# Attention and a routed expert layer in one kernel: four stores per stretch moved one place, seven places for the first units' layers, list work moved inside a layer, and a different last scaling

## The chip, the cores and the metric

The kernel runs on one core of one Trainium2 chip. The metric is the device time of one execution in microseconds; of the kernel before there are three timed runs and one profiled execution.

## The reference, cut to what matters

```python
# attention, for each of 8 batches and 8 heads, 576 positions, 64 numbers per head
scores = q @ k.T / 8;  cum = cumsum(max(s, 0))
attn = softmax(where(causal, -1e9, scores + min(-(cum_i - cum_j), 0)))
x = (attn @ v) with the heads side by side                # 8 x 576 tokens of 512 numbers
# experts: 8 of them, w1[e] is 512 x 1024, w2[e] is 1024 x 512
logits = x @ w_gate
e[s] = argmax(logits[s]) if s == 0 or sigmoid(x[s] @ w_local) < 0.5 else e[s - 1]
out[s] = softmax(logits[s])[e[s]] * (max(x[s] @ w1[e[s]], 0) @ w2[e[s]])
```

Each token goes through one expert, and which one depends on the tokens before it in its batch.

## The kernel before, in words

**Attention** runs over 16 slots (`m` in `attention`). A slot takes two head pairs, `a` and `b`. TensorE first makes the scores of both (`ps`, line 1129); ScalarE turns them into exponentials `e` (line 1130), and GpSimd blanks the part above the diagonal (line 1113). TensorE then makes the diagonal blocks of the next slot's scores (`ph`, line 1147) and, for both pairs, the products with the values (`po` for `a`, `pb` for `b`, lines 1186 and 1198), each in two parts. VectorE divides each part by its sums (`recs`, `xb`, line 1208). `ph`, `po` and `pb` are many small matrix products of 64 columns; the scores are fewer and larger ones.

A slot has numbered places at which other work may be planned: 0 and 1 after the scores of `a` and `b`, 3 after the values of `a`, 4 after the values of `b`, 5 after VectorE's turning and weighting work. Four batches of tokens have been finished after eight slots, and so on: after every four slots a **group** of two batches is routed (`Router`: small products `lp`, line 231, and `pos`, line 316, and many small VectorE operations), and its 18 pieces of 128 half rows are stored into a table in DRAM, ordered by expert. Such a **store** is an indirect DMA that GpSimd issues (`put`, line 364), and ahead of each stands a one-element copy or memset into `gap` (lines 361 and 363) that makes it wait for something: in attention for a `recs` value of its place, later for the ScalarE result of its step. The table `STORES` says at which place of which slot each store stands. Stores of the third group that have no place there go into a list, `experts.puts`. The fourth group's 18 stores and 8 more (`pads`) join that list when the fourth group is routed (`late_rows`).

**Experts** runs 20 units of tokens of one expert each, `ORDER = "PPDDDDDDDDDDTDDRMDRR"`: most have 256 tokens, the last ones fewer. The phases are (1, 0), then (1, u), (2, u-1) for u = 1 to 19, then (2, 19), where (1, u) is the first layer of unit u and (2, u) its second. In `SPLIT` layers (both layers of D and R units, the second of P units) a layer is seven products of half size instead of eight, `layer_split`: products 1, 2, 6, 7, 5, 4, 3 in that order, with sums and differences of weights (`wt`, and in place `w1b`, `w2b`: `weight_first` to `weight_fourth`, line 618, VectorE) and of rows (`row_sums`, `row_fourth`, lines 663 to 669, GpSimd, or VectorE for the first layer of the first five units). After each product VectorE adds it up (`sa`, `sb`, `sc`, `hT`, `y`, line 712), and `at(0)` to `at(6)` run the work planned at that place. Such work, for other units, is planned with `job`, which cuts a place to the number of places a layer has. That number is in `steps`; for the second layer of a P unit it says 2, although that layer runs as a split one with seven places:

```python
steps = {"P": (FK, 2), "D": (7, 7), "R": (7, 7), "M": (2, 1), "T": (2, 1)}
plan(what, u, i if i == "pre" else min(i, steps[self.kind(u)][what - 1] - 1), lambda: f(*args))
```

At each place one store is taken from `experts.puts`. Which units hold whole doubles of which expert is computed in lists: `assign_early(0)` in attention slot 11 for the first `EARLY[0]` units, `assign_early(1)` in phase (1, 0) for the next `EARLY[1]`, `assign_doubles` in (1, 1), and `assign_rest`, a chain of 18 steps of one to five tiny VectorE operations, that starts with phase (2, 3). The rows of a unit are fetched from the table by SyncE (`fetch`, line 583), after every store that stands ahead of it in the program has landed, and the weights by SyncE (`load`, line 573). SyncE works in order.

At the end, the last layer's last product is added into `y` by VectorE, scaled by the gate `gi` on ScalarE (line 716) and stored with an indirect DMA from GpSimd (line 757).

Of the kernel before, what the change touches and what calls it, by code (L numbers as in the profile page):

```python
# [12 lines left out]
Alu = mybir.AluOpType  # L13
# [40 lines left out]
STORES = (((3, 5, 5, 5, 5), (3, 5, 5, 5, 5), (5, 5, 5, 5), (5, 5, 5, 5)), ((3, 5, 5, 5, 5), (3, 5, 5, 5, 5), (5, 5, 5, 5), (5, 5, 5, 5)),  # L54
          ((3, 4, 5, 5, 5, 5), (3, 5, 5, 5, 5)))
# [8 lines left out]
EARLY = (2, 3)  # L64
# [3 lines left out]
LOOK, REST_FROM, REST_STEP = 5, 8, 3  # L68
# [434 lines left out]
class Experts:  # L503
# [191 lines left out]
    def layer_split(self, u, layer, at):  # L695
# [48 lines left out]
        at(5, ins)  # L744
        p3 = self.product(u, layer, 3)
        add(c12, p3, s2)
        ins = last(c12, 0)
# [63 lines left out]
    def run(self, recs, wend, out_of):  # L811
# [61 lines left out]
        def late_rows():  # L873
            assert not self.puts
            router.ranks(last, self.banks)
            router.rows(last)
            router.gates(last, self.xb)
            self.puts += [lambda behind, c=c: router.scatter(last, c, behind=behind) for c in range(NC)]
            self.puts += router.pads()
# [8 lines left out]
        plan(1, 1, 2, lambda: loads(0), late_rows)  # L888
# [12 lines left out]
        steps = {"P": (FK, 2), "D": (7, 7), "R": (7, 7), "M": (2, 1), "T": (2, 1)}  # L901
# [5 lines left out]
        for u in range(end):  # L907
            if u >= 2:
                job(2, u - 2, "pre" if u > 2 else 1, turn_x, u)
            for layer in range(2):  # L910
                if not self.split(u, layer):
                    continue
                if layer:
# [6 lines left out]
                    if u < 2:  # L920
                        place = ((1, 1), (2, 0))[u] + ("pre",)
# [19 lines left out]

        def fetches():
            nonlocal fetched
            while fetched < min(end, turned + 2):
                stored = not self.puts
                if (1, 1, 2) in todo:
                    stored = stored and fetched < first
                elif fetched < first:
                    stored = True
                if not stored or self.table_of(*self.units[fetched][1][-1]) is None:  # L950
                    return
                self.fetch(fetched)
                fetched += 1
# [9 lines left out]
        def step(what, u):  # L963
            def at(i, ins=None):
                self.relu = ins or self.relu
                run_plan(what, u, i)
                if now >= REST_FROM and (7 * now + i) % REST_STEP == 0:
                    next(rest, None)
                if self.puts and (now or i > 2) and (now != 2 or i % 2 == 0):
                    self.puts.pop(0)(self.relu)  # L970
                fetches()
                free()
# [956 lines left out]
```

## Time and profile before

| | us |
|---|---|
| three timed runs | 697.51, 697.1, 700.85 |
| their median | 697.51 |
| profiled execution, time | 704.64 |
| its span from the first to the last instruction | 702.8 |
| TensorE busy | 678.5 |
| VectorE busy | 526.1 |
| GpSimd busy | 382.1 |
| ScalarE busy | 198.9 |

The profiled execution is 7.1 us over the median and 1.8 us over its own span. In its timeline the attention slots begin at 9.6 us and are some 11 us long, longer from the seventh on; the first expert phase begins at 212.0 us, (2, 0) at 242.6, (1, 2) at 257.1, and from there a phase takes some 12.3 us.

### The profile page before, as it was taken

How to read it: one execution, taken by the hardware profiler on the slowest of the kernel's cores; microseconds unless marked ns; L12 is line 12 of the kernel's file. 1: busy time of each engine (PE TensorE's matmuls, PEld its weight loads, DVE VectorE, ACT ScalarE, POOL GpSimd, SP SyncE). 2: the span in 40 equal slices, each digit the busy share in tenths (PEclk: the TensorE clock that was granted, in tenths of full speed). 3: DMA queues.
4: the chain of work that ended last, by engine and by line, in shares of the span. 5: the costliest groups of instructions: out<-in, count | busy, mean ns of one | idle time of the engine just before them, and what ended most of it. 6: DMA issues, size and time to landing. Idle time of an engine off the chain costs nothing.

```text
span 702.8 us, 19163 instructions
## 1 busy us (share of the span) xinstructions
PE 678.5 (97%) x7837; PEld 586.0 (83%) x7837; DVE 526.1 (75%) x979; ACT 198.9 (28%) x368; POOL 382.1 (54%) x547
## 2 busy tenths in 40 slices
PE   8999999989989989999999999999999999999995
PEld 6787877777768879999998999999777998679984
DVE  4655846876867588889989998887659686778763
ACT  4545436435421211212212122221211112111121
POOL 3552366766754768853654557456243482535742
PEclk9999999999999999999999999999999999999998
DMA  7664555656558589679876468166989898866001
GB/s 255 202 220 131 173 183 157 220 188 208 188 139 350 174 303 352 207 272 351 294 270 212 141 247 280 47 235 205 301 288 375 337 337 279 284 265 253 31 9 42
DMA packets 54968, 158.18 MB, mean 225 GB/s; under 512 B 11156, under 2 KB 31636, under 8 KB 49111
## 3 DMA queue, kind: packets, MB, share of 16 engines
q1 hardware_dynamic: 47751, 136.52, 57.2%
q0 software_dynamic: 6880, 20.10, 7.5%
q8 instruction: 64, 1.05, 0.6%
q14 instruction: 33, 0.27, 0.1%
q10 hardware_dynamic: 240, 0.25, 0.1%
HBM read 136.21 MB, written 20.85 MB: 223 GB/s over the span
## 4 chain that ended last, share of the span: by engine, by line
PE 88%; DVE 4%; issue 3%; DMA 3%; POOL 1%; ACT 1%; POOLq 0%; DVEq 0%
PE p L688 27%; PE p L692 26%; PE ps L1129 10%; PE po L1186 6%; PE pb L1186 6%; PE hp L782 4%; PE hp L773 2%; PE yp L805 2%; PE ph L1147 2%; PE lp L231 2%; DMA w1b<-in_w_dram 2%; PE po L1198 1%; DVE wt L618 1%; DMA qb<-in_q_dram 1%; PE pb L1198 1%
## 5 line engine op out<-in xcount | busy, mean ns | idle before, releaser
L692 PE MATMUL p<-w2b,hT 128*128 128x256 f32 (+1 forms) x720 | 164.9, 380 | 3.1 <-POOL gap L361 2.0
L692 PEld LDWEIGHTS p<-w2b,hT 128*128 128x128 f32 (+1 forms) x720 | 132.8, 187 | 25.7 <-issue 3.4
L688 PE MATMUL p<-xT,w1b 128*128 128x128 f32 (+1 forms) x1280 | 151.2, 275 | 1.3 <-DMA w1b<-in_w_dram 0.7
L688 PEld LDWEIGHTS p<-xT,w1b 128*128 128x128 f32 x1280 | 147.8, 192 | 4.3 <-issue 1.6
L1130 ACT ACTIVATE e<-ps 128x768 f32<-128x768 f32 (+1 forms) x96 | 76.9, 884 | 62.9 <-PE ps L1129 55.0
L757 POOL DMA_INDIRECT out_dram<-y,gi x38 | 44.7, 1175 | 82.2 <-ACT y L716 74.5
L716 ACT ACTIVATE y<-y,gi 128x256 f32<-128x256 f32 (+1 forms) x72 | 35.5, 506 | 167.5 <-DVE y L712 152.4
L717 ACT ACTIVATE hT<-hT 128x512 f32<-128x512 f32 (+1 forms) x64 | 39.0, 616 | 152.5 <-DVE hT L712 152.5
L1129 PE MATMUL ps<-qb,kb 64*128 64x384 f32 (+4 forms) x516 | 76.6, 441 | 2.3 <-DVE xb L1208 1.5
L669 POOL TENSOR_TENSOR hT<-hT,hS 128x512 f32<-128x512 f32 (+1 forms) x18 | 26.1, 1450 | 87.5 <-PE p L692 87.4
L1129 PEld LDWEIGHTS ps<-qb,kb 64*128 64x128 f32 x516 | 47.0, 186 | 29.5 <-ACT e L1130 8.7
L692 PE MATMUL p<-wt,hS 128*128 128x256 f32 (+1 forms) x288 | 68.0, 379 | 0.0
L364 POOL DMA_INDIRECT table<-xb,idx x54 | 58.2, 1077 | 14.6 <-issue 13.3
L688 PE MATMUL p<-xS,wt 128*128 128x128 f32 (+1 forms) x512 | 62.4, 275 | 0.0
L692 PEld LDWEIGHTS p<-wt,hS 128*128 128x128 f32 (+1 forms) x288 | 53.8, 187 | 8.4
L688 PEld LDWEIGHTS p<-xS,wt 128*128 128x128 f32 x512 | 59.7, 192 | 0.0
L1113 POOL TENSOR_SCALAR_AFFINE_SELECT e<-e 128x128 f32<-128x128 f32 (+1 forms) x96 | 33.6, 375 | 39.3 <-ACT e L1130 39.0
L1186 PE MATMUL pb<-vg,e 128*64 128x66 f32 x1280 | 41.3, 222 | 1.1 <-issue 1.0
L1186 PE MATMUL po<-vg,e 128*64 128x66 f32 x1280 | 42.0, 226 | 0.0
L1186 PEld LDWEIGHTS po<-vg,e 128*64 128x64 f32 x1280 | 39.7, 141 | 1.2
L1186 PEld LDWEIGHTS pb<-vg,e 128*64 128x64 f32 x1280 | 39.4, 138 | 1.7 <-issue 1.3
L665 POOL TENSOR_TENSOR hT<-hT 128x512 f32<-128x512 f32 (+1 forms) x18 | 36.4, 2020 | 0.0
(290 smaller groups left out, 998.3 us busy)
## 6 DMA issues: line engine op xcount, KB each, us to landing
w2b<-in_w_dram SPq DMA_DIRECT2D x23, 2048.0 KB
w1b<-in_w_dram SPq DMA_DIRECT2D x22, 2048.0 KB
va<-in_v_dram SPq DMA_DIRECT2D x32, 320.0 KB
kb<-in_k_dram SPq DMA_DIRECT2D x31, 288.0 KB
qb<-in_q_dram SPq DMA_DIRECT2D x31, 288.0 KB
xq<-table SPq DMA_DIRECT2D x60, 130.0 KB
w1b<-in_w_dram SPq DMA_DIRECT2D x4, 512.0 KB
xq<-table SPq DMA_DIRECT2D x12, 113.8 KB
```

The lines of the kernel that those rows point to most:

```text
L364: put = self.nc.gpsimd.indirect_dma_start(out=self.halves, in_=src, element_offset=0, in_offset=None, out_offset=bass.IndirectOffsetOnAxis ...
L665: on.tensor_tensor(a21, a11, a21, op=Alu.subtract)
L688: mm(ps[:, m * h : m * h + h], lhsT=b[:, k, m * P : m * P + P], rhs=a[:, k, :], start=m == 0 and k == 0, stop=m == FK // 2 - 1 and k == n - 1)
L692: mm(ps[:h, : D // 2], lhsT=a[:, k, :], rhs=b[:, k, :], start=k == 0, stop=k == n - 1)
L716: return nc.scalar.mul(to, to, gi[:h, r, 1:2]).ins
L717: return nc.scalar.activation(to, to, Act.Relu).ins
L757: put = nc.gpsimd.indirect_dma_start(out=self.out[:, :], out_offset=bass.IndirectOffsetOnAxis(ap=gi.bitcast(I32)[:m, n, 0:1], axis=0), in_ ...
L782: mm(ps, lhsT=self.ws[ls[0]][0][:, k, c * P : c * P + P], rhs=xT[:, k, :w], start=(k == 0), stop=(k == DK - 1))
L1113: nc.gpsimd.affine_select(out=ap, in_=ap, compare_op=Alu.is_ge, fill=0.0, base=base, pattern=n, channel_multiplier=-1)
L1129: mm(ps[:, h, at : at + z - a], lhsT=kb[d, key : key + P], rhs=qb[d, a:z], start=True, stop=True)
L1130: exps[n, u] = nc.scalar.activation(e[:, :, : WIDTH[u]], ps, Act.Exp, scale=scale).ins
L1186: of = mm(po[part][d, j - a, :], lhsT=weights_of(n, c, j, h), rhs=vgs[n % NV][:, c if j < 2 * G1 else G1 + c, h, :], start=(first and i == ...
```

## The change

Five things are edited.

- `STORES`: in the eight slots of groups 0 and 1, one store moves from place 5 to place 4. Group 2 had 11 stores in its two attention slots and now has 5, so 13 instead of 7 go to `experts.puts`, which then holds up to 39 instead of 33 over the phases. Stores are taken at all places of phase (1, 0) but the third, where before they were taken from the fourth on.
- `steps` says 7 for the second layer of P units, so work planned at later places of (2, 0) and (2, 1) stays there; two row sums get new places with it, and `loads(0)` moves from place 2 to place 1 of (1, 1).
- `EARLY` is (4, 1) instead of (2, 3), and `fetches` lets units 0 to 3 be fetched as soon as phase (1, 1) begins, without waiting for the list of stores to be empty.
- `assign_rest` advances at places 3 and 4 of each layer instead of at each third place counted through.
- In the very last layer ScalarE scales `s2` ahead, and one VectorE operation scales the last product and adds.

```diff
-STORES = (((3, 5, 5, 5, 5), (3, 5, 5, 5, 5), (5, 5, 5, 5), (5, 5, 5, 5)), ((3, 5, 5, 5, 5), (3, 5, 5, 5, 5), (5, 5, 5, 5), (5, 5, 5, 5)),
-          ((3, 4, 5, 5, 5, 5), (3, 5, 5, 5, 5)))
+STORES = (((3, 4, 5, 5, 5), (3, 4, 5, 5, 5), (4, 5, 5, 5), (4, 5, 5, 5)), ((3, 4, 5, 5, 5), (3, 4, 5, 5, 5), (4, 5, 5, 5), (4, 5, 5, 5)),
+          ((4, 5, 5, 5), (4,)))
...
-EARLY = (2, 3)
+EARLY = (4, 1)
...
-LOOK, REST_FROM, REST_STEP = 5, 8, 3
+LOOK, REST_FROM, REST_AT = 5, 8, (3, 4)
...
+        end = u == len(self.units) - 1
+        if layer and end:
+            nc.scalar.mul(s2, s2, gi[:h, 0, 1:2])
         p3 = self.product(u, layer, 3)
-        add(c12, p3, s2)
-        ins = last(c12, 0)
+        if layer and end:
+            ins = nc.vector.scalar_tensor_tensor(c12, p3, gi[:h, 0, 1:2], s2, Alu.mult, Alu.add).ins
+        else:
+            add(c12, p3, s2)
+            ins = last(c12, 0)
...
-        plan(1, 1, 2, lambda: loads(0), late_rows)
+        plan(1, 1, 1, lambda: loads(0))
+        plan(1, 1, 2, late_rows)
...
-        steps = {"P": (FK, 2), "D": (7, 7), "R": (7, 7), "M": (2, 1), "T": (2, 1)}
+        steps = {"P": (FK, 7), "D": (7, 7), "R": (7, 7), "M": (2, 1), "T": (2, 1)}
...
-                        place = ((1, 1), (2, 0))[u] + ("pre",)
+                        place = ((1, 1, "pre"), (2, 0, 2))[u]
...
+        def group_stored():
+            return len(self.puts) <= (0 if (1, 1, 2) in todo else NC + E)
+
         def fetches():
             nonlocal fetched
             while fetched < min(end, turned + 2):
-                stored = not self.puts
-                if (1, 1, 2) in todo:
-                    stored = stored and fetched < first
-                elif fetched < first:
-                    stored = True
-                if not stored or self.table_of(*self.units[fetched][1][-1]) is None:
+                stored = fetched < EARLY[0] or (fetched < first and group_stored()) or not ((1, 1, 2) in todo or self.puts)
+                if not now or not stored or self.table_of(*self.units[fetched][1][-1]) is None:
                     return
...
-                if now >= REST_FROM and (7 * now + i) % REST_STEP == 0:
+                if now >= REST_FROM and i in REST_AT:
                     next(rest, None)
-                if self.puts and (now or i > 2) and (now != 2 or i % 2 == 0):
+                if self.puts and (now, i) != (0, 2) and (now != 2 or i % 2 == 0):
                     self.puts.pop(0)(self.relu)
```

What this does to the order of instructions shows at three places. The lines of the changed kernel are up to five higher than those of the kernel before. TensorE's and SyncE's rows stay as they were but for the list from which a unit's number is read.

First, GpSimd around the border of slots 8 and 9: the masks of slot 8, then four stores of group 0, then the first masks of slot 9. Before:

```order
L1113 AFFINE_SELECT eh<-eh 128x640
L363 COPY gap<-recs 1x1
L364 DMA table<-w2b,idx 75264x260
L361 MEMSET gap 1x1
L364 DMA table<-w2b,idx 75264x260
L361 MEMSET gap 1x1
L364 DMA table<-w2b,idx 75264x260
L361 MEMSET gap 1x1
L364 DMA table<-w2b,idx 75264x260
L1113 AFFINE_SELECT e_2274<-e_2274 128x2x64
```

And in the changed kernel:

```order
L1118 AFFINE_SELECT eh<-eh 128x640
L363 COPY gap<-recs 1x1
L364 DMA table<-w2b,idx 75264x260
L363 COPY gap<-recs 1x1
L364 DMA table<-w2b,idx 75264x260
L361 MEMSET gap 1x1
L364 DMA table<-w2b,idx 75264x260
L361 MEMSET gap 1x1
L364 DMA table<-w2b,idx 75264x260
L1118 AFFINE_SELECT e_2274<-e_2274 128x2x64
```

The order of stores and masks is the same. The first store now waits for the first part of `pb` and the second for its second part, where before the first waited for the second part and the others followed it.

Second, VectorE in phase (2, 0), from the fourth weight difference (`w2b<-w2b,wt`) to the last addition (`sb` and `sc` are sums of products, `y` the results, `xT` and `xS` the rows of unit 2, `wt` with `w1b` the weights of unit 2, `wt` with `w2b` those of unit 1). Before:

```order
L618 TENSOR_TENSOR w2b<-w2b,wt_4268 128x4x256
L618 TENSOR_TENSOR wt_4311<-w2b 128x1024
L604 STREAM_TRANSPOSE xT<-xq 128x8x4x32
L663 TENSOR_TENSOR xS<-xT 128x256
L664 TENSOR_TENSOR xS<-xS,xT 128x256
L665 TENSOR_TENSOR xT<-xT 128x2x128
L618 TENSOR_TENSOR wt_4319<-w1b 128x1024
L618 TENSOR_TENSOR wt_4319<-w1b,wt_4319 128x1024
L712 TENSOR_TENSOR sb_4337<-p_4332,sa_4298 128x256
L712 TENSOR_TENSOR sc_4346<-p_4341,sb_4337 128x256
L712 TENSOR_TENSOR sb_4337<-p_4348,sb_4337 128x256
```

And in the changed kernel:

```order
L618 TENSOR_TENSOR w2b<-w2b,wt_4260 128x4x256
L604 STREAM_TRANSPOSE xT<-xq 128x8x4x32
L712 TENSOR_TENSOR sb_4316<-p_4311,sa_4286 128x256
L712 TENSOR_TENSOR sc_4329<-p_4324,sb_4316 128x256
L663 TENSOR_TENSOR xS<-xT 128x256
L664 TENSOR_TENSOR xS<-xS,xT 128x256
L665 TENSOR_TENSOR xT<-xT 128x2x128
L712 TENSOR_TENSOR sb_4316<-p_4335,sb_4316 128x256
L712 TENSOR_TENSOR y<-p_4335,sc_4329 128x256
L618 TENSOR_TENSOR wt_4343<-w1b 128x1024
L712 TENSOR_TENSOR y<-p_4347,sc_4329 128x256
L618 TENSOR_TENSOR wt_4358<-w2b 128x1024
```

The additions moved ahead of the row sums and of three weight differences for units 1 and 2. On GpSimd, in the same phase, the last row difference `hT<-hT,hS` of unit 0 moved ahead of the three row sums `hS`, `hS`, `hT` of unit 1, as the next pieces show. Before:

```order
L663 TENSOR_TENSOR hS<-hT 128x512
L664 TENSOR_TENSOR hS<-hS,hT 128x512
L665 TENSOR_TENSOR hT<-hT 128x4x128
L361 MEMSET gap 1x1
L364 DMA table<-xb,idx 75264x260
L669 TENSOR_TENSOR hT<-hT,hS 128x4x128
```

And in the changed kernel:

```order
L361 MEMSET gap 1x1
L364 DMA table<-xb,idx 75264x260
L669 TENSOR_TENSOR hT<-hT,hS 128x4x128
L663 TENSOR_TENSOR hS<-hT 128x512
L664 TENSOR_TENSOR hS<-hS,hT 128x512
L665 TENSOR_TENSOR hT<-hT 128x4x128
```

The row difference no longer stands behind them.

Third, VectorE at the beginning of phase (2, 5), where before four list operations (`dstep`, `dpast`) stood between the turned rows of a later unit and the first addition. Before:

```order
L618 TENSOR_TENSOR wt_5278<-w1b,wt_5278 128x1024
L409 TENSOR_SCALAR dstep<-n_f 128x8
L411 TENSOR_TENSOR dstep<-dstep,start 128x8
L412 TENSOR_TENSOR dstep<-dstep,start 128x7
L413 TENSOR_TENSOR dpast<-dpast,dstep 128x24
L712 TENSOR_TENSOR y<-p_5323,sa_5316 128x256
L618 TENSOR_TENSOR w2b<-w2b,wt_5166 128x4x256
```

And in the changed kernel:

```order
L618 TENSOR_TENSOR wt_5269<-w1b,wt_5269 128x1024
L712 TENSOR_TENSOR y<-p_5309,sa_5307 128x256
L618 TENSOR_TENSOR w2b<-w2b,wt_5166 128x4x256
L712 TENSOR_TENSOR sb_5327<-p_5322,sa_5307 128x256
L618 TENSOR_TENSOR w1b<-w1b 128x2x512
```

The four operations moved behind the addition of product 5 of the same phase.

More of the change, by code (lines that the diff above doesn't have):

```diff
@@ L873, in late_rows @@
         def late_rows():
-            assert not self.puts
             router.ranks(last, self.banks)
```

## The prediction

> **What bounds the kernel now.** I read the page's busy times first: the row gives each engine's busy microseconds, the share of the span and the number of instructions.
>
> ```profile
> PE 678.5 (97%) x7837; PEld 586.0 (83%) x7837; DVE 526.1 (75%) x979; ACT 198.9 (28%) x368; POOL 382.1 (54%) x547
> ```
>
> TensorE is the bound. The change takes no matrix product away, so it can win only what TensorE waits. The waits of TensorE come next: microseconds in total, times, longest.
>
> ```profile
> PE ph L1147 <- issue: 5.0, 11, 1.0
> PE p L692 <- POOL gap L361: 2.0, 1, 2.0
> PE lp L231 <- issue: 2.0, 6, 0.4
> PE ps L1129 <- DVE xb L1208: 1.5, 1, 1.5
> PE p L692 <- DVE w2b L618: 1.1, 1, 1.1
> PE p L688 <- DVE w1b L618: 0.6, 1, 0.6
> ```
>
> Two kinds: short waits in attention that no semaphore explains ("issue"), some 8.5 us with the `ps` row, and three waits in the expert phases, 3.7 us. The busy times of whole attention slots say more, since a slowed TensorE counts as busy. Below: a slot without stores, then slots 7, 9 and 13, which do the same matrix products and have stores. The columns are the stretch, its length, the busy times of TensorE, its weight loads, VectorE, ScalarE and GpSimd, the granted clock, the DMA share and GB/s.
>
> ```profile
> 30.66:41.66 11.00, 11.00 (x274) 9.11 (x274) 6.08 (x14) 5.76 (x10) 6.73 (x29) 1.00 0.62 187
> 88.98:104.36 15.38, 14.00 (x274) 11.38 (x274) 6.08 (x14) 5.88 (x10) 9.71 (x19) 0.89 0.58 181
> 171.59:183.85 12.26, 11.29 (x275) 9.26 (x274) 10.30 (x35) 6.09 (x11) 7.78 (x16) 1.00 0.73 236
> ```
>
> A slot with stores costs 1.3 us more (12.26 - 11.00), once 4.4 us, with the granted clock at 0.89.
>
> **Term 1, the stores in attention.** The timeline of slot 13 shows the last two of its four stores (GpSimd, line 364), and `ph` stopping after 11 of 40 records; two rows of slot 9 follow. Below them, from slots 11 and 9: a store beside the values `pb`, and `pb` with that store and without one.
>
> ```profile
> 174.84 0.97 POOL L364 DMA_INDIRECT table<-xb,idx  x1 [0.22 <-issue]
> 176.11 0.96 POOL L364 DMA_INDIRECT table<-xb,idx  x1 [0.23 <-issue]
> 176.48 0.39 PE L1147 MATMUL ph<-qb,kb 64*64 64x64 f32 x11
> 177.84 0.73 PE L1147 MATMUL ph<-qb,kb 64*64 64x64 f32 x29 [0.96 <-issue]
> ...
> 123.15 0.96 POOL L364 DMA_INDIRECT table<-w2b,idx  x1 [0.23 <-issue]
> 124.88 0.71 PE L1147 MATMUL ph<-qb,kb 64*64 64x64 f32 x28 [0.94 <-issue]
> 155.24 1.00 POOL L364 DMA_INDIRECT table<-xb,idx  x1 [0.16 <-issue]
> 154.40 2.76 PE L1186 MATMUL pb<-vg,e 128*64 128x66 f32 x79
> 128.25 2.50 PE L1186 MATMUL pb<-vg,e 128*64 128x66 f32 x80
> ```
>
> TensorE goes on 0.77 us after the store's end (176.11 + 0.96 = 177.07; 177.84), and 0.77 after it in slot 9 (123.15 + 0.96 = 124.11; 124.88). I take the stores as the cause, though the trace names none. A store takes 1.27 us with its memset (176.11 - 174.84). With one store of the four moved ahead into the values, the last one ends at 175.8, before `ph` begins at 176.48, and 0.77 us later is 176.57: the wait of 0.96 is nearly all gone. In slot 7 the waits come in a row and would only begin earlier and end earlier. In the last two slots six stores leave altogether. From above, all `ph` and `lp` waits go: 5.0 + 2.0 = 7.0. I take half, 3.5, because the cause is inferred. Against it: eight stores now run beside `pb`, at 2.76 - 2.50 = 0.26 each at most, 2.1; four of the eight follow another store and reach into the scores, so I charge two, 0.5. **Term 1: -3.0**, between -7.0 and a loss that the second rival sizes.
>
> The Trainium skill, Runtime: NRT & Kernel Launch, section Instruction fetch mechanics, says that an engine streams its instructions by a DMA queue of its own, in blocks of 256, and that this is hidden by the rate at which instructions are issued. If "issue" is instructions that come late behind stores, the rows above disagree with that; by the page the waits are something else, the stores need not matter, and the sum would be 3.0 smaller. That is the first rival.
>
> **Term 2, phase (2, 0).** TensorE stops ahead of product 3 of (2, 0) and ahead of product 7 of (1, 2).
>
> ```profile
> 246.71 2.85 DVE L618 TENSOR_TENSOR w2b<-w2b,wt 128x1024 f32<-128x1024 f32 x1
> 250.65 1.27 POOL L665 TENSOR_TENSOR hT<-hT 128x512 f32<-128x512 f32 x1
> 251.48 1.52 DVE L618 TENSOR_TENSOR wt<-w2b 128x1024 f32<-128x1024 f32 x1 [1.91 <-PE p L692]
> 252.92 1.23 DVE L604 STREAM_TRANSPOSE xT<-xq 128x1024 f32<-128x1024 f32 x1
> 253.89 1.27 POOL L669 TENSOR_TENSOR hT<-hT,hS 128x512 f32<-128x512 f32 x1
> 254.26 1.20 DVE L663 TENSOR_TENSOR xS<-xT 128x256 f32<-128x256 f32 x1
> 255.22 1.99 PE L692 MATMUL p<-w2b,hT 128*128 128x256 f32 x8 [2.05 <-POOL gap L361]
> 258.56 0.42 DVE L712 TENSOR_TENSOR sb<-p,sa 128x256 f32<-128x256 f32 x1
> 261.94 1.22 DVE L618 TENSOR_TENSOR w1b<-w1b 128x1024 f32<-128x1024 f32 x1
> 263.21 2.05 PE L688 MATMUL p<-xT,w1b 128*128 128x128 f32 x16 [0.64 <-DVE w1b L618]
> ```
>
> Product 3 waits 2.05 us for the row difference of line 669, which stands behind unit 1's row sums (the last ends at 250.65 + 1.27 = 251.92) and a store. With the row sums planned two places later it stands behind the store alone; three row operations of 1.27 or more leave from ahead of it, 253.89 becomes about 250.1, its end 251.4, before the 253.17 at which TensorE began to wait. So this wait goes. VectorE has lost 1.91 us there too, waiting for product 5 so that it could overwrite `wt`; moved behind product 4's addition, that operation waits for nothing. Then VectorE decides how early product 7 of (1, 2) starts: from the end of the fourth difference (249.56) it does the transpose 1.2, two additions 0.8, row sums 2.0 (1.20 and two like the additions), two additions 0.8, a difference 1.2, an addition 0.4, two differences 2.4, an addition 0.4, and two differences 2.4, the second being the `w1b` that product 7 needs, which is 11.6, or 11.7 with a gap or two: 249.56 + 11.7 = 261.3 against 263.16. So 1.9 us; without the contention that makes the fourth difference 2.85 instead of 1.2 it would be all of 2.05 + 0.64 = 2.7. **Term 2: -2.1**, between -1.4 (half a microsecond more of contention) and -2.7. In (2, 1) the same cut of places goes; TensorE does not wait there, so 0.
>
> The earlier fetch of units 2 and 3, `EARLY` and `loads(0)` at place 1 bring transfers forward; no row of the list of waits names them, so 0, and they cover term 2: the transpose needs unit 2's rows sooner than before.
>
> **Term 3, the list.** In (2, 5) four list operations stand ahead of the fourth difference, for which product 4 waits 1.06 us.
>
> ```profile
> 374.87 0.69 DVE L409 TENSOR_SCALAR dstep<-n_f 128x8 f32<-128x8 f32 x1
> 377.34 1.21 DVE L618 TENSOR_TENSOR w2b<-w2b,wt 128x1024 f32<-128x1024 f32 x1
> 378.69 3.69 PE L692 MATMUL p<-w2b,hT 128*128 128x256 f32 x16 [1.06 <-DVE w2b L618]
> ```
>
> The four and the addition behind them take 377.34 - 374.87 = 2.47; without the four the addition's 0.4 is left, and the difference begins 2.1 us sooner. They now stand behind the additions of products 7 and 5, where only later additions follow, and the next difference is needed a phase on. **Term 3: -1.1**, from 0 (another operation is late instead) to -1.1. The lists end one or two phases later; the unit that needs the last one is fetched two phases after that.
>
> **Term 4, the six stores moved into the expert phases.** Two more fit into (1, 0), four lengthen the queue at its other end. The rows show the last of the old list, the row difference behind it, SyncE's fetch of unit 5, which waits for all stores, and products 4 and 3 of (2, 2).
>
> ```profile
> 298.79 1.09 POOL L364 DMA_INDIRECT table<-pad,pad_i  x1 [0.21 <-issue]
> 299.90 1.28 POOL L669 TENSOR_TENSOR hT<-hT,hS 128x512 f32<-128x512 f32 x1
> 302.02 1.90 SPq L583 DMA_DIRECT2D xq<-table  x4
> 303.69 3.62 PE L692 MATMUL p<-w2b,hT 128*128 128x256 f32 x16
> ```
>
> Four stores at 1.27 are 5.1 us. Product 3 starts at 303.69 + 1.8 = 305.5 and its row difference ends at 301.2: cover 4.3. But GpSimd's queue also begins earlier, since the results of (2, 0), for whose scaling it waits, come with `sb` at about 251 instead of 258.56. So I cost it at 0, between 0 and +3 (5.1 + 2.1, as TensorE comes earlier, less 4.3).
>
> **Term 5, the end.** VectorE's addition, ScalarE's scaling, the store:
>
> ```profile
> 695.26 0.42 DVE L712 TENSOR_TENSOR y<-p,sb 104x256 f32<-104x256 f32 x1 [1.30 <-PE p L692]
> 695.72 0.51 ACT L716 ACTIVATE y<-y,gi 104x256 f32<-104x256 f32 x1 [1.22 <-DVE y L712]
> 696.52 1.00 POOL L757 DMA_INDIRECT out_dram<-y,gi  x1 [0.63 <-ACT y L716]
> ```
>
> ScalarE's 0.51 leaves the path. Its new scaling of `s2` runs while TensorE does product 3. The combined operation has no row; its nearest is the addition, 0.42. **Term 5: -0.5**, between 0 and -0.8 (696.52 less 695.72).
>
> **The sum**: -3.0 - 2.1 - 1.1 + 0 - 0.5 = -6.7, on the profiled execution 704.64 to 697.9. That execution lies 7.1 over the median of 697.51; taken off the median, the sum gives **690.8 us**, 1.0% less.
>
> **The rivals.**
> First: the waits called "issue" have nothing to do with the stores. For it speaks that no semaphore ties them together; against it that in two slots they end the same 0.77 us after the last store. Then -3.7 is left: 693.8.
>
> Second, slower: the waits follow the stores. A store beside `pb`, whose products are as small as those of `ph`, costs there what it cost in `ph`: eight at 0.96 are +7.7, nothing is won in `ph`, and with -3.7 from the rest the kernel ends at 701.5. It decides from 0.46 a store on (3.7 / 8). Against it stands the one row with a store beside `pb`, 0.26.
>
> Third: the longer list of stores is late. GpSimd does not start earlier, product 3 of (2, 2) waits 3, and the time is 693.8 with term 1, about 697 without it.
>
> Fourth: the planning for (2, 0) does not do what it says, because the transpose of unit 2, now ahead of the additions, waits for rows that came no sooner; term 2 falls to 0 and the time is 692.9.
>
> **How the numbers follow.** Forecast 0.50, first rival 0.25, second 0.08, third 0.10, fourth 0.07. A change under 0.5%, 3.5 us, is about what a measurement of this kernel cannot tell from none: 694.0 and 701.0 are the bounds. Faster: the forecast and the fourth, 0.57, half of the first, whose 693.8 lies at the bound, and a little of the third, together 0.70. Slower: most of the second, 0.07. Same: the rest, 0.23. The range takes term 1 to -7 below (686.8) and the first rival with the smaller ends of the other terms above (697.5 - 1.4 - 0.5 = 695.6, with some of the third 696.5).
>
> **What would show it.** Term 1: slots 9 and 13 near 11.3 us and the `ph` total far below 5.0; if the `pb` values grow instead, the second rival. Term 2: no wait for GpSimd in (2, 0), and product 7 of (1, 2) some 2 us sooner after the start of (2, 0). Term 3: no wait for `w2b`. Term 4: the last store before 300, counted from an equal start of phase (1, 0). Term 5: the last indirect DMA follows VectorE directly. Wrong would be: `ph` waits as before, or a new wait in the phases (1, 2) to (2, 3).

## The result, and the profile after

| | median, us | ratio to before, 95% interval |
|---|---|---|
| kernel before, beside these runs | 698.55 | |
| changed kernel | 692.63 | 0.9917 (0.9890 to 0.9944) |
| changed kernel, measured again | 693.44 (before 698.40) | 0.9935 (0.9909 to 0.9960) |

By the two ratios the change saves 5.8 and 4.5 us (0.83% and 0.65% of 698.5). The first profiled execution of the changed kernel took 688.57, 4 below its median, as the one of before took 704.64, 7 above its own; so one execution against the other says too much. The rows of this section are from these first profiles; the comparisons further on use second profiles of both kernels as well.

First the busy times, then what TensorE waited for (total, times, longest) in the changed kernel's first profile:

```profile
PE 670.9 (98%) x7837; PEld 582.2 (85%) x7837; DVE 522.1 (76%) x979; ACT 199.1 (29%) x368; POOL 385.5 (56%) x547
...
PE pb L1191 <- issue: 3.6, 4, 1.5
PE p L692 <- DVE w2b L618: 1.4, 1, 1.4
...
PE po L1191 <- issue: 0.8, 2, 0.6
PE p L688 <- DVE w1b L618: 0.5, 1, 0.5
```

No `ph` or `lp` row is left, as forecast, and of GpSimd only 0.3 us ahead of the constants `cps` at the start; but `pb` and `po` now wait 4.4 us for "issue", where before they waited 1.0. Slots 2, 7 and 13, the three shown of before:

```profile
29.89:40.97 11.08, 11.08 (x274) 9.16 (x273) 6.08 (x14) 5.75 (x10) 6.82 (x29) 1.00 0.60 193
89.38:100.63 11.25, 11.20 (x276) 9.19 (x273) 6.08 (x14) 5.75 (x10) 10.04 (x21) 1.00 0.77 241
164.05:175.50 11.45, 11.20 (x276) 9.17 (x273) 10.51 (x35) 5.96 (x11) 6.93 (x16) 1.00 0.72 223
```

Slots 7 and 13 stand 0.2 and 0.4 us over the slot without stores, where before they stood 4.4 and 1.3 over it. But that is one execution against another. In slot 7 of before the granted clock was 0.50 for 3.4 us, and TensorE was busy for 14.00 us against 11.03 in that kernel's second profile. In the second profiles slots 7 and 13 take 12.03 and 11.72 us before the change and 12.37 and 11.15 after it.

In phase (2, 0) the transpose of unit 2 comes ahead, products 4 and 3 run through, and product 7 of (1, 2) follows:

```profile
237.46 1.23 DVE L604 STREAM_TRANSPOSE xT<-xq 128x1024 f32<-128x1024 f32 x1
238.50 3.62 PE L692 MATMUL p<-w2b,hT 128*128 128x256 f32 x16
...
248.04 1.16 PE L688 MATMUL p<-xT,w1b 128*128 128x128 f32 x8 [0.55 <-DVE w1b L618]
```

The last store and the row difference behind it, and the end of the kernel:

```profile
286.29 0.96 POOL L364 DMA_INDIRECT table<-pad,pad_i  x1 [0.22 <-issue]
287.28 1.60 POOL L669 TENSOR_TENSOR hT<-hT,hS 128x512 f32<-128x512 f32 x1
...
679.64 0.48 DVE L750 SCALAR_TENSOR_TENSOR y<-p,gi,sb 104x256 f32<-104x256 f32 x1 [1.37 <-PE p L692]
680.43 1.00 POOL L763 DMA_INDIRECT out_dram<-y,gi  x1 [0.22 <-issue]
```

The row difference ends at 288.88, 1.4 us before product 3 of (2, 2) starts at 290.25. At the end the store follows VectorE's start by 0.79 us, before by 1.26.

The table compares stretches between the same matrix products in all profiles (the kernel's single matrix products are numbered from 0 here and below): attention from the start of slot 1 to matrix product 4652, the sixth of (1, 0); (2, 0) from matrix product 4867, with which product 7 of (2, 0) begins, to product 7 of (1, 2); the list from product 3 of (2, 2) to product 4 of (2, 5); from there to matrix product 7011, at about 550 in the small units; and from the last matrix product's start to the span's end. The kernels are those of the experiments below.

```
us                            attention  (2,0)   list    to 550   end
before, first profile           193.57   15.38   73.28   184.23   7.93
before, second profile          186.09   14.39   73.27   184.34   7.83
before, new stores              187.50   14.32   73.28   185.03   7.94
before, new places              188.05   13.38   73.28   184.90   8.00
before, new lists and end       186.90   16.17   72.05   184.78   7.87
before, 4 extra stores          191.13   14.50   73.27   185.21   8.48
before, 8 extra stores, late    188.60   16.15   73.28   184.80   8.87
before, 8 extra, one early      187.46   16.16   73.28   184.90   8.72
changed, first profile          182.25   13.00   72.05   184.79   7.41
changed, second profile         185.54   13.01   72.05   184.23   7.71
changed, old stores             183.69   13.00   72.05   185.93   7.69
changed, old places             186.00   15.17   72.16   184.43   7.45
changed, stores still earlier   185.91   13.01   72.05   184.93   7.62
changed, old third list         184.67   12.62   72.05   184.50   7.60
```

### The profile page after: what moved, and what is told of

Same layout as the page of the kernel before. It is cut to its first block, busy times and chain, and to the rows that moved or that the text cites. A ratio compares the mean times of both kernels' runs of the same rounds, so it can differ in the third digit from the quotient of the medians.

```text
span 686.6 us, 19166 instructions
## 1 busy us (share of the span) xinstructions
PE 670.9 (98%) x7837; PEld 582.2 (85%) x7837; DVE 522.1 (76%) x979; ACT 199.1 (29%) x368; POOL 385.5 (56%) x547
## 4 chain that ended last, share of the span: by engine, by line
PE 87%; DMA 4%; DVE 3%; issue 3%; POOL 2%; ACT 1%; SPq 0%; POOLq 0%; DVEq 0%
PE p L692 28%; PE p L688 25%; PE ps L1134 10%; PE po L1191 6%; PE pb L1191 6%; PE hp L788 4%; DMA w1b<-in_w_dram 3%; PE hp L779 2%; PE lp L231 1%; PE ph L1152 1%; DMA w2b<-in_w_dram 1%; PE yp L811 1%; DVE wt L618 1%; PE po L1203 1%; DVE w2b L618 1%
## 5 line engine op out<-in xcount | busy, mean ns | idle before, releaser
L763 POOL DMA_INDIRECT out_dram<-y,gi x38 | 46.2, 1215 | 73.2 <-ACT y L716 65.1
L669 POOL TENSOR_TENSOR hT<-hT,hS 128x512 f32<-128x512 f32 (+1 forms) x18 | 24.7, 1370 | 88.8 <-PE p L692 88.7
L1118 POOL TENSOR_SCALAR_AFFINE_SELECT e<-e 128x128 f32<-128x128 f32 (+1 forms) x96 | 35.3, 392 | 39.3 <-ACT e L1135 39.0
L1111 DVE TENSOR_TENSOR vg<-va,wk 128x256 f32<-128x256 f32 x64 | 37.6, 652 | 0.0
```

The source lines that it names most:

```text
L763: put = nc.gpsimd.indirect_dma_start(out=self.out[:, :], out_offset=bass.IndirectOffsetOnAxis(ap=gi.bitcast(I32)[:m, n, 0:1], axis=0), in_ ...
L1111: nc.vector.tensor_tensor(vg[:, to].rearrange("p c h e -> p (c h) e")[:, :, :DH], va[:, :c].rearrange("p c h e -> p (c h) e"), wk[:, n, to ...
L1118: nc.gpsimd.affine_select(out=ap, in_=ap, compare_op=Alu.is_ge, fill=0.0, base=base, pattern=n, channel_multiplier=-1)
```

## The experiments

**The new stores alone**, on the kernel before, for groups 0 and 1:

```diff
-((3, 5, 5, 5, 5), (3, 5, 5, 5, 5), (5, 5, 5, 5), (5, 5, 5, 5))
+((3, 4, 5, 5, 5), (3, 4, 5, 5, 5), (4, 5, 5, 5), (4, 5, 5, 5))
```

> The kernel before, with the stores of the first two groups alone moved to the new places (one of each slot's goes from behind the last values to ahead of them); the third group, the planned layers, the lists and the end stay as before. Theory (the late stores hold up ph and lp): the ph and lp waits of slots 6 to 13 go, ph from 5.0 us to under 1.5, those of lp in slot 15 stay (about 1.0), slots 9 and 13 come to about 11.4 us, and the time is 3.0 us less than before, about 694.5 to 695.5. First rival (the waits have nothing to do with the stores): ph stays near 5.0, the time within 1 us of before. Second rival (the waits follow the stores): po and pb waits called issue grow from 1.0 to 7 or more, the time is 4 us above before.

Measured: 697.77 us, ratio 0.9983 (0.9955 to 1.0011), so -1.2 us, between -3.1 and +0.8. No `ph` wait was left; `pb` and `po` waited 8.8 us for "issue". Every theory missed something: the theory in the size, the first rival in `ph`, the second in the time.

**The new places alone**, on the kernel before:

```diff
-steps = {"P": (FK, 2), ...
+steps = {"P": (FK, 7), ...
-place = ((1, 1), (2, 0))[u] + ("pre",)
+place = ((1, 1, "pre"), (2, 0, 2))[u]
```

> The kernel before, with only the planned places of the first layers changed (seven places instead of two, row sums of unit 1 at the third place of (2, 0)); the stores, the early fetch, the lists and the end stay as before. Theory (the row difference on GpSimd stands behind the row sums): the wait for GpSimd ahead of product 3 of (2, 0), 2.05 us, goes, product 7 of (1, 2) starts about 1.9 us sooner after the start of (2, 0), and the time is 2.1 us less than before, about 695.4 to 696.4. Rival (the transpose of unit 2 waits for its rows, which are fetched only 2.8 us before the phase): VectorE waits for the rows at the transpose, the fourth difference and product 7 come no sooner, and the time is within 0.7 us of before.

Measured: 696.66 us, ratio 0.9971 (0.9944 to 0.9998), -2.0 us. The GpSimd wait was gone and (2, 0) took 13.38. The rival falls: the transpose did not wait for rows. This kernel has the old stores, and it had no `ph` wait at all; instead `po` waited 3.2 us, three times, for GpSimd's masks.

**The old stores** in the changed kernel (the first edit, reversed):

> The changed kernel, with the stores of the first two groups put back to their places before (all behind the last values of a slot but the first); the shorter third list and all else stay changed. Theory (late stores cost): the ph waits come back, 2 to 4 us in slots 7 to 13, the issue waits of pb shrink from 3.6 to about 1, and the time is 2 to 3 us above that of the changed kernel, about 695. First rival (the waits come by chance of the transfers, whatever the place of the stores): the time is within 1 us of the changed kernel's 692.6.

Measured: 695.61 us, ratio 0.9949 (0.9920 to 0.9978), some 1 to 2 us more than the changed kernel's two ratios, but with intervals that overlap. `ph` did not come back; `po` waited 2.0 us for masks. So it is not shown that late stores cost time as a whole, and if they do, it is not by the mechanism that I had named. The one profile does not show it either: attention took 183.69 us, against 185.54 in the changed kernel's second profile.

**The old places** in the changed kernel (the second edit, reversed):

> The changed kernel, with the planned places of the first layers put back (two places, row sums of unit 1 ahead of (2, 0)); the stores, the early fetch, the lists and the end stay changed. Theory (places give term 2, and they also start GpSimd's list of stores sooner, which pays for the four stores more): the wait for GpSimd ahead of product 3 of (2, 0) comes back with about 2 us, and since the longer list of stores now starts as late as before, the row difference of (2, 2) ends up to 3 us late: the time is 2 us (the wait alone) to 5 us (with the late list) above the changed kernel, 694.7 to 697.7. Rival (the early fetch and the new third list alone give the gain there): no GpSimd wait over 0.5 us, the time within 0.7 us of the changed kernel.

Measured: 697.39 us, ratio 0.9977 (0.9949 to 1.0006), 3 to 4 us more than the changed kernel, within what was expected. The rows show product 3 of (2, 2) behind the row difference, and that behind the longer list of stores:

```profile
295.88 0.96 POOL L364 DMA_INDIRECT table<-pad,pad_i  x1 [0.23 <-issue]
...
296.85 1.28 POOL L669 TENSOR_TENSOR hT<-hT,hS 128x512 f32<-128x512 f32 x1
...
298.18 1.99 PE L692 MATMUL p<-w2b,hT 128*128 128x256 f32 x8 [0.98 <-POOL gap L762]
```

Only one part missed: in (2, 0) it was not product 3 that waited, but product 7 of (1, 2), 2.46 us for `w1b`.

**The kernel before, a second profile.**

> The kernel before, unchanged, for a second profile. Old theory (the stores behind the values hold up ph): the ph waits stand again in slots 7 to 14, 4 to 6 us. New theory (the ph waits belonged to that one execution, since two kernels with the old places of the stores showed none; what the late stores hold up is GpSimd's masking of the next slot's scores): no ph or lp waits called issue beyond 1 us in all, and instead po waits for GpSimd's masks 2 to 4 times by about 1 us, as in the run with the planned places alone (3.2 us, 3 times).

Measured: 695.52 us, one run. From the list of TensorE's waits:

```profile
PE po L1186 <- POOL e L1113: 3.0, 3, 1.0
PE pb L1186 <- issue: 2.7, 6, 1.2
...
PE ph L1147 <- issue: 0.3, 1, 0.3
```

The 5.0 us of `ph` waits belonged to one execution. What the late stores do in slot 7 shows in the timeline (stores on line 364, masks on line 1113); the slot begins at 90.84:

```profile
92.03 1.60 POOL L364 DMA_INDIRECT table<-w1b,idx  x1 [0.54 <-issue]
...
95.80 0.76 PE L1147 MATMUL ph<-qb,kb 64*64 64x64 f32 x40
...
96.46 0.96 POOL L364 DMA_INDIRECT table<-w1b,idx  x1 [0.22 <-issue]
...
97.44 0.91 POOL L1113 TENSOR_SCALAR_AFFINE_SELECT e<-e 128x128 f32<-128x128 f32 x3
97.79 0.62 PE L1186 MATMUL po<-vg,e 128*64 128x66 f32 x13 [1.00 <-POOL e L1113]
```

GpSimd has the masks of slot 7's exponentials behind the stores of the group; the values `po` wait for the first mask. In the changed kernel's first profile, where the slot begins at 89.38:

```profile
90.11 0.99 POOL L364 DMA_INDIRECT table<-w1b,idx  x1 [0.16 <-issue]
...
94.08 0.96 POOL L364 DMA_INDIRECT table<-w1b,idx  x1 [0.23 <-issue]
...
95.05 1.76 POOL L1118 TENSOR_SCALAR_AFFINE_SELECT e<-e 128x128 f32<-128x128 f32 x6
95.41 1.79 PE L1191 MATMUL po<-vg,e 128*64 128x66 f32 x54
```

As many stores run at this border, but the second need not wait for the last values: it starts 0.73 us into the slot instead of 1.19, the masks 5.67 into it instead of 6.60, and `po` waits for nothing.

**Extra stores, late.** The kernel before with eight stores more:

```diff
+for e, (i, p) in enumerate(((3, 5), (3, 5), (3, 5), (3, 5), (5, 5), (5, 5), (5, 5), (5, 5))):
...
+    plan(i, p, lambda e=e, after=after: router.put(router.pad, router.extra[:, e : e + 1], after))
```

> The kernel before with eight stores more, four behind the last values of slot 3 and four behind those of slot 5, which have none; they write a constant tile into rows of their own that nothing reads. New theory (masks of the next slot stand behind the stores on GpSimd): in slots 4 and 6 the first mask starts only when the fourth store has ended, about 7.0 us after the slot's scores began, and po waits for GpSimd by about 1.0 in each; the time is 1 to 2 us more. Old theory (stores hold up ph): ph or lp waits called issue appear in slots 4 and 6, 0.9 or more each, and no wait for masks. Rival (a store costs nothing as long as nobody needs its data): both slots keep 13.3 and 10.9 to 11.7 us, the time stays within 0.5 us.

Measured: 701.64 us, ratio 1.0044 (1.0020 to 1.0068), +3.1 us. The time went the first theory's way, by more than it said, but the place did not agree: the masks started 6.62 and 5.85 us into slots 4 and 6, yet `po` waited in neither, since the router's products `lp` (2.4 us) and `pos` (0.8) stand ahead of it there. The profile shows the longer time elsewhere, against the second profile of before: attention +2.5 (`pb` and `po` wait 7.0 us for "issue" instead of 4.0), (2, 0) +1.8 (told below), the end +1.0. Whether the first of these comes from the extra stores stays open. The end is longer in all three kernels with extra stores, and the trace shows where. After the last store GpSimd's `DRAIN` takes 1.06 us in every kernel with 118 indirect transfers, 1.39 with four more and 1.71 with eight more, and the `INC_SWDGE_SEM` ahead of it 0.42, 0.50 and 0.58: about 0.1 us for each extra store, though the stores themselves ran hundreds of microseconds earlier.

**Extra stores, one of four early** (the first and fifth place above are (3, 4) and (5, 4)):

> As the run with eight stores more, but one of each four stands ahead of the last values, at the place that the changed kernel uses. New theory: three stores are left in front of the masks, which start one store (1.27 us) sooner, and the waits of po for GpSimd in slots 4 and 6 are gone; the time is that of the kernel before, within 1 us. Old theory: ph waits shrink to at most 0.3 each. Rival (any store costs alike): as much above the kernel before as with the four late ones.

Measured: 699.85 us, ratio 1.0012 (0.9989 to 1.0035). The waits in slots 4 and 6 were absent already with the late ones, so this pair tells the theories apart by its time alone, and weakly: 1.8 us between the two, with intervals that overlap.

**Extra stores ahead of slot 5**, which has no router products (four, all at (4, 5)):

> The kernel before with four stores more, all behind the last values of slot 4, so that they run beside the scores of slot 5, which has no router products between scores and values that could cover a late mask (slots 4 and 6 have, and showed no wait with the extra stores). They write a constant tile into rows of their own that nothing reads. New theory: the first mask of slot 5 starts 5.9 to 6.6 us after the slot's first score instead of 2.3, and po waits for GpSimd by 0.3 to 1.1 us; slot 5 is 11.2 to 12.0 us long instead of 10.93. Old theory: a ph wait called issue of about 0.9 in slot 5. Rival (a store costs TensorE nothing): slot 5 stays at 10.93.

Measured: 699.94 us, ratio 1.0012 (0.9988 to 1.0037). Slot 5 took 12.85 us, from 66.75 on:

```profile
72.17 0.97 POOL L366 DMA_INDIRECT table<-pad,extra  x1 [0.22 <-issue]
73.16 1.75 POOL L1115 TENSOR_SCALAR_AFFINE_SELECT e<-e 128x128 f32<-128x128 f32 x6
73.51 2.55 PE L1188 MATMUL po<-vg,e 128*64 128x66 f32 x80 [0.76 <-POOL e L1115]
```

The mask starts 6.41 us into the slot and `po` waits 0.76; no `ph` wait. That is the mechanism, made at a place that has none without the extra stores. (The slot's length was missed: `pb` waited 0.82 for "issue" besides.)

**The stores still earlier** in the changed kernel:

```diff
-((3, 4, 5, 5, 5), (3, 4, 5, 5, 5), (4, 5, 5, 5), (4, 5, 5, 5))
+((3, 3, 4, 4, 5), (3, 3, 4, 4, 5), (3, 4, 4, 5), (3, 4, 4, 5))
```

> The changed kernel with the stores of the first two groups moved still further: one behind the last values of each slot, the others beside the values and the first of them beside the scores. New theory: after the change no po wait for a mask is left, so nothing more can be won; within 1 us of the changed kernel (692.6), and masks of the third scores may come late, at most 1 us a slot, which would make it 1 to 4 us slower. Old theory (each store moved ahead takes away what it cost): 1 to 2 us faster than the changed kernel.

Measured: 692.91 us, ratio 0.9907 (0.9876 to 0.9939), the same as the changed kernel. It had no mask wait to remove, and none came.

**The changed kernel again.**

> The changed kernel, unchanged, for a second profile and more runs. Old theory (the change takes away ph waits) and new theory (it takes away waits for GpSimd's masks) both expect the same time, 692 to 694; the new one expects no po wait for a mask over 0.5 us, and attention (slot 1 to the first product of phase (1, 0)) at 183 to 186 us, about 1 us less than in kernels with the old places (mean 185.9 in the three without extra stores and without ph waits), since its first profile's 182.3 was a good execution.

Measured: 693.44 us, ratio 0.9935; no mask wait, attention 185.54.

**The old third list** in the changed kernel (eleven stores beside slots 14 and 15):

> The changed kernel with the third group's list as before (eleven stores beside slots 14 and 15 in place of five; six fewer in the phases behind). New theory: four stores again stand in front of slot 15's masks, po waits for GpSimd there once, 0.5 to 1.4 us, as in all kernels with the old list; the phases behind keep their lengths (the shorter queue gains nothing, since the row difference of (2, 2) had no wait): 0.5 to 1.4 us above the changed kernel. Old theory: lp waits called issue return in slot 15, 1 to 2 us. Rival (the longer queue costs more than it gains): 1 us faster than the changed kernel.

Measured: 693.66 us, ratio 0.9946 (0.9922 to 0.9971), against 0.9935 for the changed kernel beside it. One mask wait returned in slot 15, 0.5 us, and no `lp` wait. The times cannot be told apart.

**The lists and the end alone**, on the kernel before:

> The kernel before with only the lists' places and the scaling of the last product changed. Theory by terms 3 and 5: the stretch from product 3 of (2, 2) to product 3 of (2, 5) comes from 73.28 to about 72.05, the w2b wait of 1.06 in it is gone, and the stretch behind the last matrix product comes from 7.83 to about 7.4; the time is 1.5 us less than before. Rival (given back): TensorE, which comes 1.2 us sooner, waits that much longer where VectorE makes w2b late for the smaller units, 1 to 2 us at about 550, and the time is 0.4 less.

Measured: 697.10 us, ratio 0.9993 (0.9962 to 1.0023), -0.5 us. The list's stretch took 72.05 instead of 73.27, as forecast; VectorE's start to the last store came to 0.79, though the end as a whole took 7.87; and 0.95 of waiting for `w2b` stood at 555, as the rival has it. But that wait does not come from the new lists. With the old ones it stands there too; below are the new stores alone and the new places alone, with the list's 1.06 and, as the second wait in each row, 0.95 and 1.22 at about 555:

```profile
PE p L692 <- DVE w2b L618: 2.0, 2, 1.1
PE p L692 <- DVE w2b L618: 2.3, 2, 1.2
```

It is absent in four profiles alone (both of before, the second of the changed kernel, and the old places), the same four in which TensorE had waited 0.7 to 1.1 us for the transfer of `w1b` ahead of matrix product 6699, at 513 to 525 us; in the others it waited 0.5 or less for it.

Besides, (2, 0) took 16.17, against 14.39 in the second profile of before. These rows are from (2, 0), first of this kernel, then of the second profile of before:

```profile
244.09 3.08 DVE L618 TENSOR_TENSOR wt<-w2b 128x1024 f32<-128x1024 f32 x1 [2.84 <-PE p L692]
...
244.80 1.27 POOL L669 TENSOR_TENSOR hT<-hT,hS 128x512 f32<-128x512 f32 x1
...
256.61 1.60 PE L688 MATMUL p<-xT,w1b 128*128 128x128 f32 x12 [2.46 <-DVE w1b L618]
```

```profile
243.33 1.22 DVE L618 TENSOR_TENSOR wt<-w2b 128x1024 f32<-128x1024 f32 x1 [2.83 <-PE p L692]
...
244.05 1.63 POOL L669 TENSOR_TENSOR hT<-hT,hS 128x512 f32<-128x512 f32 x1
...
254.06 2.05 PE L688 MATMUL p<-xT,w1b 128*128 128x128 f32 x16 [0.98 <-DVE w1b L618]
```

The two operations hold each other up. Either GpSimd's is stretched (1.63) and VectorE's takes 1.22, or GpSimd's takes 1.27 and VectorE's lasts until GpSimd's end (244.80 + 1.27 = 246.07) and 1.10 more. In the three kernels with 3.06 to 3.08 the stretch took 16.15 to 16.17, in the three with 1.22 or 1.23 it took 14.32 to 14.50; the two others lie between (1.52 with 15.38, 2.07 with 15.17). So with the old places (2, 0) depends on which of the two comes through.

## Why the prediction was right, and where it was wrong

Forecast 690.8, measured 692.6 and 693.4: faster, inside the range. The terms:

**Term 1, -3.0, failed in its mechanism and was too large.** The step that failed is the one from "TensorE goes on 0.77 us after the store's end" to "I take the stores as the cause". These waits belonged to one execution: the second profile has 0.3, and the kernels with the old stores and other edits have 0.3 or none. The signs that I had named for the term do not show it either, since without the change they nearly hold as well: in the second profile of before, slots 9 and 13 take 11.38 and 11.72 us, with `ph` at 0.3. What held TensorE in the first profile is open; ScalarE stood still until the same moment in slot 13 (177.97 against 177.84). What late stores do hold up is GpSimd, which I had not followed past the store: the masks of the next slot are queued behind it, 2.0 to 3.2 us of `po` waits in the four kernels with the old stores, no extra ones and no `ph` waits, 0 to 0.5 in those with the new ones. The stores ahead of slot 5 show that this is so.

Most of this gain is given back in the same slot. In slot 11 of the second profiles, before and then changed:

```profile
148.09 2.55 PE L1186 MATMUL po<-vg,e 128*64 128x66 f32 x80 [1.04 <-POOL e L1113]
...
151.23 1.97 PE L1186 MATMUL pb<-vg,e 128*64 128x66 f32 x60 [0.18 <-issue]
```

```profile
147.59 2.55 PE L1191 MATMUL po<-vg,e 128*64 128x66 f32 x80
...
151.56 2.14 PE L1191 MATMUL pb<-vg,e 128*64 128x66 f32 x66 [1.01 <-issue]
```

The slots begin at 141.10 and 141.71. `po` starts 6.99 and 5.88 us into them, a gain of 1.11; after the wait of `pb`, 93 products on, TensorE stands at 10.13 and 9.85, a gain of 0.28. The `pb` wait stands ahead of matrix product 3392 in both, and it has the same place in nearly all profiles:

```
wait in us ahead of    product 3299 (mask)   product 3392 (issue)
before, 2nd profile          1.04                  0.18
before, new places           1.03                  0.19
changed, old stores          1.03                  none
before, new lists, end       1.04                  0.18
changed, 1st / 2nd profile   none                  0.73 / 1.01
before, new stores           none                  0.74
changed, old places          none                  1.29
changed, still earlier       none                  0.46
changed, old third list      none                  1.01
```

These "issue" waits look like late instructions. No run moved one, so this is argued from their places and times. They recur ahead of the products numbered 853, 1106, 1360, 1996, 2249, 2503, 2885, 3139, 3392, 3645, 4028, 4281 and 4536, which lie 253 to 255 apart, or 1.5 or 2.5 times that. In ten profiles there were 82 waits at these products, and 79 of them ended 1.2 to 1.6 us after a packet of 16,384 bytes of the instruction queue had landed: in the changed kernel's second profile landing at 150.25 and wait until 151.56, 138.47 and 139.93, 161.85 and 163.17. The landings themselves are 4 to 8 us apart there. On this reading, whoever comes sooner to such a border waits there.

The stores alone gave -1.2 (-3.1 to +0.8), and attention took 185.3 on average in six profiles with the new stores, against 186.2 in four with the old ones and neither extra stores nor `ph` waits. But the six run from 182.3 to 187.5 and the four from 183.7 to 188.1, so the 0.9 between them is not clear of the spread: that the masks come sooner is shown, that the kernel gains by the stores is not. The first rival, that the "issue" waits have nothing to do with the stores, fits the second profiles, though it did not have the masks; its -3.7 is about as near to the measured -4.5 and -5.8 as the forecast's -6.7, so the time does not decide between them. The second was right that waits of `pb` take the place of others (4.8 us of `pb` and `po` "issue" waits on average in those four, 6.6 in the six), but by their places they belong to the borders and not to the store beside them, and the kernel did not become slower.

The prediction cited the Trainium skill, Runtime: NRT & Kernel Launch, section Instruction fetch mechanics, by which instructions are streamed in blocks of 256 and crossing a block's border is mostly hidden. A product is two instructions here, a weight load and a multiplication, so 254 products are 508 instructions, about two such blocks, which agrees. If the waits are such crossings, they are not hidden for these small products: 4.4 us of waits in the changed kernel's first profile, 8.8 with the new stores alone.

**Term 2, -2.1, right**: 15.38 to 13.00 between the first profiles, and 15.28 on average in the eight with the old places against 13.00 in the six with the new ones: -2.3. It hangs on what each execution does with the old places (14.3 to 16.2), so the gain runs from 1.3 to 3.2, wider than my -1.4 to -2.7; I had the contention of VectorE and GpSimd in the lower bound as half a microsecond, and it is up to 1.8. Nor did that contention go: in the changed kernel's first profile the fourth difference takes 3.61 us (until 237.54, which is the end of the second GpSimd operation beside it, 236.45, and 1.09 more), and the stretch 13.0; in the run with the old third list it takes 1.22, and the stretch 12.62. The Trainium skill, SBUF — State Buffer, section SBUF: two separate sides, says that VectorE and GpSimd share a pair of ports that one instruction holds as a whole while the other stands still. The 3.08 = until GpSimd's end and 1.10 more agree. That the instruction which starts first gets the pair, as the section has it too, cannot be read from the rows: VectorE's record starts at 244.09, ahead of GpSimd's at 244.80, and yet VectorE is the one that is held up. The fourth rival fell: the transpose waited for no rows.

**Term 3, -1.1, right**: -1.22 (73.27 to 72.05) in every kernel with the new list but the one with old places (72.16). But I did not ask where TensorE's lead would end, and the runs do not show it. Up to matrix product 7011, at about 550, the seven profiles with the old lists took 184.8 us on average (184.2 to 185.2) and the seven with the new ones 184.8 (184.2 to 185.9), so no part that is given back stands out. In most profiles of both kinds VectorE waits for weights there, and TensorE for VectorE; the rows are of the first profile of the changed kernel:

```profile
539.44 1.22 DVE L618 TENSOR_TENSOR wt<-w2b 128x1024 f32<-128x1024 f32 x1 [3.69 <-DMA w2b<-in_w_dram]
...
547.09 1.97 PE L692 MATMUL p<-w2b,hT 128*128 128x256 f32 x8 [1.39 <-DVE w2b L618]
```

**Term 4, 0, right, for the reason given**: the longer list ended with 1.4 us to spare because GpSimd's queue starts sooner with the new places, and without them the third rival's wait was there, 0.98 us. So the parts are not independent: the places gave -2.0 alone and 3 to 4 inside the change, and though the intervals of these two overlap, the 0.98 us of waiting stands in the rows.

**Term 5, -0.5, right**: 0.47 from VectorE's start to the last store (1.26 to 0.79).

By stretches, means over these profiles: attention -0.9, (2, 0) -2.3, list -1.2, to 550 nothing, end -0.3, together -4.7, against -4.5 and -5.8 measured. The forecast of -6.7 was too large by 0.9 to 2.2, and term 1 is what was too large: -3.0, against -0.9 by attention's means, -1.2 for the stores alone, and 1.0 to 2.2 lost with the old stores put back, none of which is clear of noise. The total came out well because terms 2, 3 and 5 did. It is luck that half of the 7.0, taken because the cause was only inferred, came this near to what the stores may be worth: the mechanism was another.

## What to carry to other kernels

Before a wait without a named releaser carries a term, see whether it is in a second profile: nearly 7 us of this one were gone, and the waits for masks showed only there. The granted clock of a single slot belongs to this look too. Follow an engine's queue past the instruction that is moved: what stood behind the stores, masks that TensorE needs, was the cost, and not the stores' neighbours on TensorE. A wait that is removed counts only as far as the next point that holds TensorE anyway (here a wait 93 products on), so look there for what is given back. And before a wait further on is called the price of a gain, see whether it stands in the kernels without the gain.

## What the runs showed of the hardware that I had not expected

With products of 128x66, about 32 ns each (80 in 2.55 us), TensorE waited 0.14 to 1.8 us ahead of fixed products with no releaser in the trace, in 79 of 82 cases until 1.2 to 1.6 us after a 16,384-byte packet of the instruction queue had landed. A VectorE operation of 1.22 us took 3.08 beside a GpSimd operation of 1.27, or the GpSimd one took 1.63 instead, and the same program did the one in one kernel and the other in another, with 1.8 us between them for the phase. Each extra indirect store of GpSimd made the kernel's end some 0.1 us longer (`DRAIN` 1.06, 1.39 and 1.71 us with 118, 122 and 126 of them).
